# Zero fills and mask rows planned as tasks, identity made in bf16 by GpSimd, first loads reordered, boot weights booked at 300 GB/s

## Chip, cores, metric

One core of one Trainium2 chip. The metric is the device time of one execution in microseconds (us). PE is TensorE, DVE VectorE, ACT ScalarE, POOL GpSimd, SP the SyncE queue that issues the loads; PEld is PE's loading of weights.

## The reference

Two transformer-like layers, each a recurrent attention with memory (A) and a gated feed-forward (B), both layers with the same weights:

```python
def _A_ref(x, mem0, Wq, Wk, Wv, Wo, seg_len):       # 2048 rows, 64 segments of 32, 32 heads of 128
    mem = mem0                                       # 8 rows
    for s in range(n_seg):
        h = concatenate([mem, x[:, s*seg_len:(s+1)*seg_len]], axis=1)      # 40 rows
        q, k, v = h@Wq, h@Wk, h@Wv
        p = softmax(where(mask, q@k.T * scale, -1e9))
        o = (p @ v) @ Wo
        mem = o[:, :M]                               # the next segment waits for this
        outs.append(o[:, M:])
x = x + _A_ref(_layernorm(x), ...);  x = x + _B_ref(_layernorm(x), ...)
x = x + _A_ref(_layernorm(x), ...);  x = x + _B_ref(_layernorm(x), ...)
```

## The kernel before

All work is given as tasks to a planner written in Python. It knows each task's engine, booked duration and dependencies, runs 24 rounds of list scheduling and fixes one order of instructions for each engine. On the chip every engine then works through its order and goes on as soon as its semaphores allow; the booked times have no part in that. So a booked number changes the order, never a duration.

The constants were made outside the plan, in an order chosen by the framework:

```python
def setup_consts(self):
    identf = fview(self.st[1][:, 0, 0:1], [(1, P)])
    cmasks.make_identity(nc, identf)                          # f32, GpSimd
    nc.vector.tensor_copy(out=self.ident[:], in_=identf)      # cast to bf16, VectorE
    ...                                                       # masks by GpSimd, small memsets by VectorE
    nc.sync.dma_start(out=self.maskb[L:LW, :], in_=self.mask1[:])
    for t_ in self.hT: nc.vector.memset(t_[:, :, L:2 * L], 0.0)
    for t_ in self.pb: nc.vector.memset(t_[:], 0.0)
    for k, t_ in enumerate(self.vsb):                         # five tiles of 128 x 1024 bf16
        self.pl.add("POOL", 950, lambda t_=t_: nc.gpsimd.memset(t_[:], 0.0), w=[...])
```

The boot loads 16 MiB of weights while PE projects V for the first twelve blocks of x ("V fill", line 570) and, as each group of six heads comes in, does Q and K of step 0:

```python
def load_weights(self):
    for h0 in range(0, self.H, 8):                            # Wv in four pieces of 1 MiB
        ld(self.wv[:, :, cs], ..., P * self.DC * 8 * P * 2 / 300.0, ...)
        for b in xb[:3]: self.load_x(b, *self.boot_x[b])
        xb = xb[3:]
    for g, (h0, gsz, us) in enumerate(self.groups):           # five groups of 6 heads, one of 2
        for nm, sb, v in (("wq", self.wq, wq_v), ("wk", self.wk, wk_v)):
            ld(sb[:, :, cs], v[:, :, cs], nb / 260.0, ...)    # booked ns: bytes / (GB/s)
        ld(self.wo[:, h0:h0 + gsz, :], ..., P * gsz * self.D * 2 / 200.0, ...)

def boot(self):                                               # priority of a boot load
    self.nboot = getattr(self, "nboot", 0) + 1
    return 1e7 - 1e4 * self.nboot

def layernorm_T(self, xb, xkey, ...):                         # bn_stats, bn_aggr, +eps on VectorE,
    ...                                                       # pow(-0.5) on GpSimd, normalise on VectorE,
                                                              # four transposes on PE with the identity
```

## Time and profile before

| | before |
|---|---|
| time, median (lowest to highest) | 1872.28 us (1869.12 to 1873.32), 3 runs |
| span of the profiled run | 1869.7 us |
| PE busy | 1822.6 us, 97% |
| PE idle, 0 to 20 us / 20 to 90 us / after 90 us | 10.7 / 0.9 / 35.5 us |
| first V matmul | 11.65 us |

The idle time of PE is the span less its busy time; the stretches come from the windows view. Not all of it is idle: this trace lacks 214 of PE's 41282 matmul records. Windows of before, from 120 to 150 us (stretch, length, busy us of PE, PEld, DVE, ACT, POOL with counts, granted clock, DMA share, GB/s):

```profile
120.00:130.00 10.00, 8.78 (x249) 7.65 (x246) 7.71 (x29) 6.10 (x23) 2.60 (x4) 1.00 0.26 69
140.00:150.00 10.00, 9.42 (x246) 8.52 (x243) 5.44 (x22) 5.58 (x20) 0.00 (x0) 0.66 0.13 35
```

PE lacks 1.2 us of 120 to 130, and in 140 to 150 the granted clock is 0.66: the trace's clock records have half clock (PE's array granted half of its full clock) from 142.0 to 148.8 us.

### The profile page before, as it was taken

Reading aid. Unit: us, or ns where it says so; the run is one execution under the profiler, and the core shown is the slowest. Engines: PE = TensorE matmul, PEld = TensorE weight load, DVE = VectorE, ACT = ScalarE, POOL = GpSimd, SP = SyncE. Lnnn points to the kernel's source line nnn. Section 1 sums busy time; section 2 is a strip of 40 time slices with the busy share of each in tenths; the row PEclk is TensorE's granted clock in tenths of the full one; section 3 lists DMA queues with packets and bytes.
Section 4 is the critical chain, followed back from the end, with each engine's and each line's share of the span. In section 5 each row is a group of like instructions: output and inputs, shape, how many; then the busy total and the mean of one; then the engine's idle time right before and its main releaser. Section 6 shows DMA issues by size and latency. Waiting matters only on the chain.

```text
span 1869.7 us, 94235 instructions
## 1 busy us (share of the span) xinstructions
PE 1822.6 (97%) x41068; PEld 1577.4 (84%) x41282; DVE 1282.3 (69%) x4167; ACT 1137.3 (61%) x2692; POOL 583.2 (31%) x832
## 2 busy tenths in 40 slices
PE   7999999999999999999999999999999999999999
PEld 3578788888989898989988898989889898988787
DVE  5366577776777667776677677666777677766565
ACT  4655556666666666566666666666666666666554
POOL 5412012332423232333323233233323232333323
PEclk9999999999999999999999999999999999999999
DMA  9733334554645544555545554555545454455534
GB/s 354 247 102 103 89 86 119 153 155 129 182 124 153 151 143 124 151 151 149 166 128 152 147 143 131 141 152 153 157 121 152 136 156 122 141 152 145 158 100 138
DMA packets 130060, 273.83 MB, mean 146 GB/s; under 512 B 29254, under 2 KB 60750, under 8 KB 129646
## 3 DMA queue, kind: packets, MB, share of 16 engines
q0 software_dynamic: 59984, 184.49, 33.7%
q1 hardware_dynamic: 69662, 83.30, 15.5%
q8 instruction: 323, 5.29, 1.2%
q14 instruction: 91, 0.75, 0.1%
HBM read 221.85 MB, written 27.26 MB: 133 GB/s over the span
## 4 chain that ended last, share of the span: by engine, by line
PE 92%; DVE 4%; ACT 2%; issue 1%; DMA 0%; POOL 0%; SPq 0%; ACTq 0%; DVEq 0%; POOLq 0%
PE bank L708 32%; PE bank L811 16%; PE bank L910 11%; PE bank L570 9%; PE bank L680 7%; PE bank L722 5%; PE bank L781 4%; PE bank L794 4%; PE bank L934 4%; PE bank L540 1%; DVE st L735 1%; ACT otsb L1002 1%; DVE pb L764 0%; DMA vsb<-sst 0%; PE bank L878 0%
## 5 line engine op out<-in xcount | busy, mean ns | idle before, releaser
L708 PE MATMUL bank<-hT,wq_sb 128*128 128x80 bf16 (+1 forms) x8960 | 624.2, 198 | 5.7 <-issue 1.7
L708 PE MATMUL bank<-hT,wk_sb 128*128 128x80 bf16 (+1 forms) x8960 | 622.9, 198 | 1.4 <-issue 1.4
L1002 ACT CAST qku<-bank 128x480 bf16<-128x480 f32 (+3 forms) x770 | 393.9, 512 | 265.5 <-PE bank L708 253.3
L708 PEld LDWEIGHTS <-wq_sb 128*128 128x128 bf16 x8960 | 458.1, 99 | 27.9 <-issue 8.5
L708 PEld LDWEIGHTS <-wk_sb 128*128 128x128 bf16 x8960 | 450.7, 99 | 1.6 <-issue 1.6
L735 DVE TENSOR_TENSOR st<-bank,maskb 80x240 f32<-80x240 f32 (+1 forms) x732 | 268.7, 368 | 234.5 <-PE bank L722 227.7
L811 PE MATMUL bank<-otsb,wo_sb 128*128 128x80 bf16 (+1 forms) x8960 | 371.8, 198 | 7.4 <-ACT otsb L1002 5.5
L811 PEld LDWEIGHTS <-wo_sb 128*128 128x128 bf16 x8960 | 339.7, 99 | 21.5 <-issue 10.3
L902 POOL DMA_DIRECT2D wg<-in_B_w_gate_dram x217 | 165.0, 760 | 489.4 <-PE bank L910 419.7
L1002 ACT CAST otsb<-bank 128x480 bf16<-128x480 f32 (+3 forms) x420 | 200.8, 486 | 76.7 <-PE bank L794 61.9
L928 POOL DMA_DIRECT2D wd<-in_B_w_down_dram x217 | 153.7, 710 | 256.6 <-PE bank L794 98.5
L764 DVE TENSOR_TENSOR pb<-st,rz 80x480 bf16<-80x480 f32 x348 | 205.8, 592 | 3.5
L745 ACT ACTIVATE st<-st 80x240 f32<-80x240 f32 (+3 forms) x420 | 159.8, 382 | 64.6 <-DVE st L742 62.7
L1002 ACT CAST ptsb<-bank 128x480 bf16<-128x480 f32 (+3 forms) x315 | 155.3, 499 | 65.2 <-PE bank L781 62.9
L530 POOL TENSOR_TENSOR lns<-lns,negh 128x1 f32<-128x1 f32 (+1 forms) x79 | 45.4, 576 | 449.0 <-DVE lns L529 334.7
L722 PE MATMUL bank<-qku 128*80 128x80 bf16 (+1 forms) x2240 | 176.7, 202 | 1.8 <-ACT qku L1002 0.4
L747 DVE TENSOR_REDUCE sm<-st 80x6 f32<-80x240 f32 (+3 forms) x420 | 151.7, 362 | 35.5 <-ACT st L745 33.4
L910 PE MATMUL bank<-xnT,wg 128*128 128x128 bf16 (+2 forms) x1784 | 171.8, 219 | 1.5 <-ACT xnT L1002 0.2
L910 PE MATMUL bank<-xnT,wu 128*128 128x128 bf16 (+2 forms) x1784 | 171.2, 218 | 0.1
L722 PEld LDWEIGHTS <-qku 128*80 128x80 bf16 (+1 forms) x2240 | 129.9, 117 | 46.2 <-issue 11.5
L903 POOL DMA_DIRECT2D wu<-in_B_w_up_dram x217 | 162.5, 749 | 4.6 <-PE bank L781 1.4
L742 DVE TENSOR_TENSOR st<-st,mx 80x240 f32<-80x240 f32 (+3 forms) x420 | 155.7, 371 | 3.9
(98 smaller groups left out, 2475.1 us busy)
## 6 DMA issues: line engine op xcount, KB each, us to landing
wg<-in_B_w_gate_dram POOLq DMA_DIRECT2D x220, 256.0 KB, 4.3
wu<-in_B_w_up_dram POOLq DMA_DIRECT2D x220, 256.0 KB, 4.7
wd<-in_B_w_down_dram POOLq DMA_DIRECT2D x220, 256.0 KB, 5.2
vsb<-scr SPq DMA_DIRECT2D x508, 48.0 KB
vsb<-sst SPq DMA_DIRECT2D x280, 64.0 KB
scr<-vst SPq DMA_DIRECT2D x128, 96.0 KB
wv_sb<-in_A_Wv_dram SPq DMA_DIRECT2D x4, 1024.0 KB
wq_sb<-in_A_Wq_dram SPq DMA_DIRECT2D x5, 768.0 KB
```

Of the source, the lines that this page charges most:

```text
L570: nc.tensor.matmul(B[:, :], lhsT=tile[:, c, :], rhs=self.wv[:, c, cs], start=(c == 0), stop=(c == DC - 1))
L708: nc.tensor.matmul(o_ap, lhsT=W[:, c, h * P:(h + 1) * P], rhs=mv(c), start=(c == 0), stop=(c == DC - 1))
L722: nc.tensor.matmul(s_all(SB)[pr, uh - h0 + i, :], lhsT=qku[:, i, 0, 0:ncol], rhs=qku[:, i, 1, 0:ncol], start=True, stop=True)
L735: pl.add("DVE", dve_ns(n, True), lambda gsz=gsz, hs=hs, st=st, SB=SB, pj_=pj_, npj_=npj_, mk=mk, idx=idx: nc.vector.tensor_tensor(out=st[p ...
L742: pl.add("DVE", dve_ns(n), lambda gsz=gsz, hs=hs, st=st, mx=mx: nc.vector.tensor_tensor(out=st[pr, hs], in0=st[pr, hs], in1=mx[pr, hs].uns ...
L745: pl.add("ACT", act_ns(n), lambda hs=hs, st=st: nc.scalar.activation(out=st[pr, hs], in_=st[pr, hs], func=ACTF.Exp, scale=self.scale), r=s ...
L764: nc.vector.tensor_tensor(out=o, in0=st[pr, hs].unsqueeze(1).to_broadcast([npart, 2, gsz, L]), in1=rz[pr, :, 0:gsz].unsqueeze(3).to_broadc ...
L811: nc.tensor.matmul(WB[:, c * ncol:(c + 1) * ncol], lhsT=self.wo[:, h, c * P:(c + 1) * P], rhs=otsb[:, hl, 0:ncol], start=(h == 0 and c == ...
L902: pl.add("POOL", 760, lambda wg=wg, fs=fs: nc.gpsimd.dma_start(out=wg[:], in_=self.wgv[:, :, fs]), r=[("wo", self.H - 1)], w=[gk] + bt, la ...
L903: pl.add("POOL", 760, lambda wu=wu, fs=fs: nc.gpsimd.dma_start(out=wu[:], in_=self.wuv[:, :, fs]), r=[("wo", self.H - 1)], w=[uk] + bt, la ...
L910: nc.tensor.matmul(gu[:, 2 * i + k, 0:n], lhsT=W[:, c, i * P:(i + 1) * P], rhs=xnT[:, c, rw], start=(c == 0), stop=(c == DC - 1))
L1002: nc.scalar.copy(out=dst, in_=src)
```

## The change

Intent: let the first layernorm start as soon as x is there, not behind constants; let the planner see the zero fills; ask for x before Wv; and book the weights' loads at a truer rate. Cut to its core:

```diff
 def setup_consts(self):
-        identf = fview(self.st[1][:, 0, 0:1], [(1, P)])
-        cmasks.make_identity(nc, identf)
-        nc.vector.tensor_copy(out=self.ident[:], in_=identf)
+        cmasks.make_identity(nc, self.ident[:])
 ...
-        nc.sync.dma_start(out=self.maskb[L:LW, :], in_=self.mask1[:])
-        for t_ in self.hT: ...  for t_ in self.pb: ...  for k, t_ in enumerate(self.vsb): ... gpsimd.memset
+    def clear(self):
+        pl.add("SP", 430, lambda: nc.sync.dma_start(out=self.maskb[L:LW, :], in_=self.mask1[:]), w=["maskb"])
+        for k, t_ in enumerate(self.hT): pl.add("DVE", 120, ... memset ...)
+        for k, t_ in enumerate(self.pb): pl.add("DVE", 400, ... memset ...)
         for k, t_ in enumerate(self.vsb):
+            if k == 0:
+                pl.add("DVE", 550, lambda t_=t_: nc.vector.memset(t_[:], 0.0), w=keys)
+            else:
+                pl.add("ACT", 960, lambda t_=t_: nc.scalar.copy(out=t_[:], in_=self.vsb[0][:]), r=[("vs", 0)], w=keys)
 def load_weights(self):
-        for h0 in range(0, self.H, 8):
+        for h0, n in ((0, 4), (4, 4), (8, 8), (16, 8), (24, 8)):        # first piece of Wv halved
-                ld(sb[:, :, cs], v[:, :, cs], nb / 260.0, ...)          # Wq, Wk
-            ld(self.wo[...], ..., P * gsz * self.D * 2 / 200.0, ...)
+                ld(sb[:, :, cs], v[:, :, cs], nb / 300.0, ...)
+            ld(self.wo[...], ..., P * gsz * self.D * 2 / 300.0, ...)
 def trace(self):
-        self.load_mem0()
+        self.clear()
         p0 = self.pre1(0); p1 = self.pre1(1)                            # loads of x0, x1
 ...
+        self.load_x(2, *self.boot_x[2])
+        self.load_mem0()
         self.load_weights()
 def run(self):
-        self.setup_consts()
         self.trace()
         order = self.pl.plan()
         with self.tc.manual_schedule():
+            self.setup_consts()
```

The rest of the diff: the first loads are booked with a latency of 2.5 us in place of 4, and the mask addition reads the key `maskb` when two layers run together.

More of the change, by code (lines that the diff above doesn't have):

```diff
@@ L465, in setup_consts @@
         nc.vector.memset(self.jm[0:L, 1:2], 0.0)
-        for t_ in self.hT:
-            nc.vector.memset(t_[:, :, L:2 * L], 0.0)
-        for t_ in self.pb:
-            nc.vector.memset(t_[:], 0.0)
-        for k, t_ in enumerate(self.vsb):
-            self.pl.add("POOL", 950, lambda t_=t_: nc.gpsimd.memset(t_[:], 0.0), w=[("vs", k), ("vx", 0, k), ("vx", 1, k)])
+    def clear(self):
+        nc, pl = self.nc, self.pl
+        pl.add("SP", 430, lambda: nc.sync.dma_start(out=self.maskb[L:LW, :], in_=self.mask1[:]), w=["maskb"])
+        for k, t_ in enumerate(self.hT):
+            pl.add("DVE", 120, lambda t_=t_: nc.vector.memset(t_[:, :, L:2 * L], 0.0), w=[("hT", k, 1, q) for q in ("m", "x")])
+        for k, t_ in enumerate(self.pb):
+            pl.add("DVE", 400, lambda t_=t_: nc.vector.memset(t_[:], 0.0), w=[("pb", k)])
+        for k, t_ in enumerate(self.vsb):
+            keys = [("vs", k), ("vx", 0, k), ("vx", 1, k)]
+            if k == 0:
+                pl.add("DVE", 550, lambda t_=t_: nc.vector.memset(t_[:], 0.0), w=keys)
+            else:
+                pl.add("ACT", 960, lambda t_=t_: nc.scalar.copy(out=t_[:], in_=self.vsb[0][:]), r=[("vs", 0)], w=keys)
     def load_weights(self):
@@ L481, in ld @@
             pl.add("SP", ns, lambda: nc.sync.dma_start(out=dst, in_=src), w=keys, boost=self.boot())
-        xb = list(self.boot_x)
-        for h0 in range(0, self.H, 8):
-            cs = slice(h0 * P, (h0 + 8) * P)
-            ld(self.wv[:, :, cs], wv_v[:, :, cs], P * self.DC * 8 * P * 2 / 300.0, [("wv", h) for h in range(h0, h0 + 8)])
+        xb = list(self.boot_x)[1:]
+        for h0, n in ((0, 4), (4, 4), (8, 8), (16, 8), (24, 8)):
+            cs = slice(h0 * P, (h0 + n) * P)
+            ld(self.wv[:, :, cs], wv_v[:, :, cs], P * self.DC * n * P * 2 / 300.0, [("wv", h) for h in range(h0, h0 + n)])
+            if h0 == 0:
+                continue
             for b in xb[:3]:
@@ L493, in load_weights @@
             for nm, sb, v in (("wq", self.wq, wq_v), ("wk", self.wk, wk_v)):
-                ld(sb[:, :, cs], v[:, :, cs], nb / 260.0, [(nm, h) for h in range(h0, h0 + gsz)])
-            ld(self.wo[:, h0:h0 + gsz, :], wo_v[:, h0:h0 + gsz, :], P * gsz * self.D * 2 / 200.0, [("wo", h) for h in range(h0, h0 + gsz)])
+                ld(sb[:, :, cs], v[:, :, cs], nb / 300.0, [(nm, h) for h in range(h0, h0 + gsz)])
+            ld(self.wo[:, h0:h0 + gsz, :], wo_v[:, h0:h0 + gsz, :], P * gsz * self.D * 2 / 300.0, [("wo", h) for h in range(h0, h0 + gsz)])
     def boot(self):
@@ L504, in load_mem0 @@
         m0 = self.xo[0][0:MEM, :]
-        pl.add("SP", 100, lambda: nc.sync.dma_start(out=m0, in_=self.mem0), w=[("xo", 0)], boost=self.boot())
+        pl.add("SP", 100, lambda: nc.sync.dma_start(out=m0, in_=self.mem0), w=[("xo", 0)], lat=2500.0, boost=self.boot())
         B = pl.buf(self.bank, "bg")
@@ L622, in pre1 @@
         xb = self.xs[i]
-        pl.add("SP", 430, lambda: nc.sync.dma_start(out=xb[:], in_=self.x_in[b * P:(b + 1) * P, :]), w=[("xs", i)], boost=(self.boot() if b < 2 else 0))
+        pl.add("SP", 430, lambda: nc.sync.dma_start(out=xb[:], in_=self.x_in[b * P:(b + 1) * P, :]), w=[("xs", i)], lat=2500.0 if b < 2 else None, boost=(self.boot() if b < 2 else 0))
         self.xw[(0, b)] = i
@@ L737, in emit_step @@
                     in1=mk[pj_, :].unsqueeze(1).to_broadcast([npj_, gsz, L]), op=ALU.add),
-                    r=[SB] + ([("st", gi, 0)] if both and j == 0 else []), w=[("st", gi, 0), ("st", gi, 1)])
+                    r=[SB] + ([("st", gi, 0)] if both and j == 0 else []) + (["maskb"] if both else []), w=[("st", gi, 0), ("st", gi, 1)])
             sk = [("st", gi, 0), ("st", gi, 1)]
```

## The prediction

> **What bounds the kernel now.** I read the page first, then busy time by windows, then the timeline of the first 24 us, then PE's waits and the SP queue. The page says that TensorE (PE) is busy for nearly the whole span, and that only the first of 40 slices is poor:
>
> ```profile
> PE 1822.6 (97%) x41068; PEld 1577.4 (84%) x41282; DVE 1282.3 (69%) x4167; ACT 1137.3 (61%) x2692; POOL 583.2 (31%) x832
> PE   7999999999999999999999999999999999999999
> PE 92%; DVE 4%; ACT 2%; issue 1%; DMA 0%; POOL 0%; SPq 0%; ACTq 0%; DVEq 0%; POOLq 0%
> ```
>
> The chain that ended last is 92% PE. So the time is PE's work, about 1822.6 us, plus PE's idle time, 1869.7 - 1822.6 = 47.1 us. The change takes no matmul away, so it can gain only in those 47 us. The windows say where they lie (columns: stretch, its length, then busy us of PE, PEld, DVE, ACT, POOL, granted clock, DMA share, GB/s):
>
> ```profile
> 0.00:10.00 10.00, 0.74 (x8) 0.60 (x8) 7.72 (x26) 1.28 (x1) 6.75 (x18) 1.00 0.78 262
> 10.00:20.00 10.00, 8.54 (x39) 3.74 (x38) 6.54 (x23) 5.13 (x14) 4.10 (x8) 1.00 1.06 374
> 20.00:30.00 10.00, 9.89 (x72) 4.43 (x72) 3.51 (x10) 5.74 (x10) 8.11 (x14) 1.00 1.07 385
> 60.00:70.00 10.00, 9.89 (x100) 5.19 (x100) 3.14 (x10) 6.30 (x13) 5.28 (x10) 1.00 0.97 317
> 70.00:80.00 10.00, 9.84 (x105) 5.54 (x105) 4.53 (x11) 5.46 (x12) 5.04 (x10) 1.00 0.64 187
> ```
>
> The first 20 us hold 10.7 us of idle PE. From 20 to 90 us, while weights arrive at up to 385 GB/s, PE lacks only 0.9 us of 70, because the V projections (line 570) fill it. From 90 us on the remaining 35 us of idle time are spread thinly over the recurrence and its end, which the change does not edit. The timeline of the first microseconds (start, duration, engine, line) shows why PE starts late:
>
> ```profile
> 1.21 0.84 SPq L623 DMA_DIRECT2D xs<-in_A_x_dram  x2
> 1.78 1.19 DVE L469 MEMSET pb<- 80x384 uint32 x3
> 3.00 3.38 DVE L451 CAST ident<-st 128x128 bf16<-128x128 f32 x1
> 3.57 2.73 POOL L471 MEMSET vsb<- 128x1024 bf16 x3
> 6.43 0.24 PE L513 MATMUL bank<-ident,xo 8*128 8x8 bf16 x4 [6.43 <-DVE ident L451]
> 6.81 1.28 DVE L527 BATCH_NORM_STATS2 lns<-xs 128x6 f32<-128x512 bf16 x2
> 9.50 0.61 PE L540 MATMUL bank<-ident,xn 128*128 128x128 bf16 x4 [2.82 <-DVE xn L531]
> 11.65 3.60 PE L570 MATMUL bank<-wv_sb,xvf 128*128 128x512 bf16 x8 [0.36 <-ACT xvf L1002]
> 16.20 2.76 PE L570 MATMUL bank<-wv_sb,xvf 128*128 128x512 bf16 x12 [0.53 <-ACT xvf L1002]
> ```
>
> What to see: casting the identity to bf16 occupies VectorE from 3.00 to 6.38 us, which is absurd for 128 elements a row. GpSimd's zero fills of vsb end at 6.30, and the cast ends 0.08 us later. Only then do the statistics of the first layernorm begin (6.81), and the first useful matmul follows 4.84 us after them, at 11.65.
>
> **What the Trainium skill says.** "SBUF — State Buffer", section "SBUF: two separate sides", says that VectorE and GpSimd share a port pair as an exclusive lock held for a whole instruction, and names an fp32 copy between SBUF tiles as an operation that takes it. The trace agrees as far as it goes: the cast lasts exactly as long as the GpSimd fills (0.08 us over), although VectorE's own memsets beside the first fill (0.12 us each) are undisturbed. "VectorE: DVE Perf Modes", section "Zero memsets can be issued as uint32 (trn2)", says that a memset takes one cycle per element and that a bf16 zero fill can be issued as half as many uint32. The trace agrees: 384 uint32 took 0.38 us. "TensorE: Matmul & The Clock Gate", section "What's actually happening", says that the array runs at half its clock for about 3.4 us of its first sustained work. The trace shows that as well: the first 8 matmuls of 512 columns took 3.60 us (0.45 each), the next 12 took 2.76 us (0.23 each). The page's granted clock reads 1.00 there, so that row does not show it. This price is paid before and after; it starts sooner when PE starts sooner.
>
> **Part by part.**
> (1) Identity in bf16 by GpSimd. Removes the cast of 3.38 us and its wait. Memset and select were 0.20 + 0.29 us in f32, so the identity is ready at about 1.3 us. Beside other work, on no path.
> (2) Zero fills. GpSimd loses five fills of 0.94 us. VectorE gets one of 512 uint32, by the row of pb 0.38 x 512/384 = 0.5 us; ScalarE gets four copies, planned at 0.96 us. ScalarE's first real work was at 10.15 us, its table load ended at 2.03, so the 3.8 us lie in a hole; at worst one copy holds up the first eviction by under 1 us. VectorE has then, before the statistics: five tiny memsets until about 1.15, eight of hT (0.58/6 each, 0.8 us), three of pb (1.19 us), one of vsb (0.5 us), so it is free at about 1.15 + 2.5 = 3.65 us. The plan will put them there: it books 0.96 + 1.2 + 0.55 = 2.7 us for them and x at 2.93.
> (3) Loads. x0 is issued at 0.75 rather than 1.21. The 8 KB of mem0, issued at 0.75, released PE's weight load at 2.39, so 1.64 us; 128 KB at 371 GB/s (the rate in the fifth microsecond) add 0.35 us. Estimate: x0 landed at 3.2 before and at 2.75 after. It was never what the statistics waited for. The first half megabyte of Wv follows three x blocks and is in by about 5.5 us, before PE can use it. The mask row's transfer leaves the front of the SP queue, where it had waited 0.6 us for GpSimd.
> So the statistics start at max(2.75, 3.65) = 3.65, not 6.81: 3.2 us sooner. With the measured 4.84 us from there, the first V matmul comes at 8.5, not 11.65. Block 2 now arrives before Wv rather than behind it, so I take back half of the 0.9 us that PE idles between 15.28 and 16.20: 0.5 us. Sum on the path: 3.7 us.
> (4) Boot weights planned at 300 GB/s. This moves no byte, it only changes where the planner puts Q/K work among the V fill. Three transfers of 768 KB are booked as 7.9 us in place of 10.0. Adding up the SP queue's bytes in the trace, the Q/K weights of the six head groups are in at about 24, 33, 42, 51, 60 and 62 us; PE uses them at 32.6, 42.9, 53.7, 64.0, 73.6 and 80.1. So they lay waiting for 9 to 19 us. With 2.1 us less per group the use moves to roughly 28, 37, 45, 53, 61 and 65: still behind the arrivals, the fifth by about 1 us. Step 0 ends some 12 us sooner and V fill is left over for steps 1 to 5, where PE idled 3.9 us between 100 and 200 us. I take 0.8 us for it.
> Total 3.7 + 0.8 = 4.5 us: 1872.3 - 4.5 = 1867.8 us, or 0.24%.
>
> **The rivals.**
> *The new plan gives it back.* Every position after the boot is planned again from other numbers, and the order of several thousand tasks can fall better or worse. For it: PE's thin idle time after 90 us is 35 us, and a tenth more or less of it is 3.5 us, as much as the gain. Against: the tasks are the same and the planner keeps the best of 24 rounds. It would make 1864 to 1872, and I expect this term to decide how close I am.
> *DMA bounds the boot.* If the last weights set the end of step 0, a sooner start only means waiting for them. For it: DMA share 1.06 from 10 to 60 us, and the SP queue blocks on issue (one Wq transfer took 5.82 us to be accepted):
>
> ```profile
> 24.78 5.82 SPq L481 DMA_DIRECT2D wq_sb<-in_A_Wq_dram  x1
> 53.12 4.04 SPq L481 DMA_DIRECT2D wq_sb<-in_A_Wq_dram  x1
> 59.13 2.11 SPq L481 DMA_DIRECT2D wo_sb<-in_A_Wo_dram  x1
> ```
>
> Against: PE was at 98% and more in those stretches, and used weights long after they came. But 300 GB/s is over what the queue gave in fact: a Wq issue ended every 9.1 us on average (20.7, 30.6, 40.2, 48.1, 57.2), that is 2.36 MB at 259 GB/s, with the scratch writes beside it. If the new order asks too early, PE waits in place and idles 2 to 4 us between 45 and 65 us, and the time stays at 1870 to 1872.
> *The fills come late.* If VectorE's or ScalarE's fills land in front of the statistics or of the first evictions, the start is at 9.5 rather than 8.5, and the time is 1869.
>
> **Range and chances.** Centre 1867.8. The front is sure to 1 us, the weights' order to 2, the new plan to 4; together about 5 us each way, with somewhat more room below since the planner now has truer numbers: 1860 to 1873.5. Two per cent would be 37 us, nearly all of the idle time that there is; so faster 0.01, slower 0.01, same 0.98.
>
> **What would show it right or wrong.** In the profile after: no cast of the identity; statistics of x at about 3.7 us; first line-570 matmul at 8 to 9 us, with slow matmuls for the 3.5 us behind it; PE busy in 0 to 20 us up from 9.3 to some 12.8; Q/K of the fifth group near 61 us without an idle stretch over 1 us before it; PE's busy total the same within 2 us of 1822.6. Wrong if the start moves by less than 2 us, if PE waits for weights between 40 and 70 us, or if idle time after 90 us moves from 35 us by more than 4.

## The result

| | before | after |
|---|---|---|
| first comparison, median (range) | 1872.53 (1869.12 to 1873.32), 4 runs | 1870.62 (1869.75 to 1871.98), 4 runs |
| ratio, 95% interval | | 0.9994, 0.9977 to 1.0011 |
| span of the profiled run | 1869.7 | 1868.4 |
| PE idle, 0 to 20 / 20 to 90 / after 90 us | 10.7 / 0.9 / 35.5 | 8.7 / 1.2 / 38.2 |
| first V matmul | 11.65 | 8.60 |

A ratio here is the mean time of one kernel's fast runs over that of the other's of the same rounds, so it is not quite the ratio of the medians. The two later comparisons of the same kernel gave 0.9987 (0.9975 to 1.0000) and 0.9995 (0.9981 to 1.0009). In means that is 1.1, 2.3 and 1.3 us less (4, 6 and 6 runs), weighted by runs 1.7 us, or 0.09%. "Same" in the sense of 2%; most likely a little faster.

The page after, the lines that answer to those of before (busy, the 40 slices of PE, the chain that ended last):

```profile
PE 1820.4 (97%) x41062; PEld 1575.1 (84%) x41282; DVE 1282.3 (69%) x4175; ACT 1140.0 (61%) x2688; POOL 576.6 (31%) x821
PE   8999999999999999999999999999999999999998
PE 88%; DVE 3%; SPq 3%; DMA 2%; issue 2%; ACT 1%; POOL 0%; ACTq 0%; DVEq 0%; POOLq 0%
```

PE's share of the chain has fallen by four points, and SPq (the queue that issues the loads) and DMA, both 0% before, now have five. The windows after:

```profile
0.00:10.00 10.00, 2.87 (x16) 1.30 (x16) 6.99 (x35) 6.95 (x12) 2.98 (x14) 1.00 0.78 264
10.00:20.00 10.00, 8.47 (x42) 3.84 (x42) 4.62 (x16) 4.19 (x8) 5.70 (x10) 1.00 1.06 382
60.00:70.00 10.00, 9.51 (x109) 5.00 (x108) 3.32 (x11) 6.13 (x13) 4.55 (x8) 1.00 1.00 330
140.00:150.00 10.00, 9.34 (x284) 7.82 (x281) 6.41 (x23) 4.34 (x16) 7.15 (x11) 1.00 0.55 156
```

The first 10 us gained 2.1 us of PE, the second 10 us nothing, 60 to 70 us lost 0.4; the half clock near 142 us is gone. The timeline after of the first microseconds:

```profile
0.74 0.87 SPq L631 DMA_DIRECT2D xs<-in_A_x_dram  x2
1.02 0.29 POOL masks.py:199 TENSOR_SCALAR_AFFINE_SELECT ident<-ident 128x128 bf16<-128x128 bf16 x1
2.42 0.48 DVE L475 MEMSET vsb<- 128x512 uint32 x1
2.94 3.88 ACT L477 COPY vsb<-vsb 128x1024 bf16<-128x1024 bf16 x4 [0.92 <-DVE vsb L475]
3.66 1.29 DVE L535 BATCH_NORM_STATS2 lns<-xs 128x6 f32<-128x512 bf16 x2
8.60 1.89 PE L578 MATMUL bank<-wv_sb,xvf 128*128 128x512 bf16 x4 [0.45 <-ACT xvf L1012]
13.60 1.33 POOL L1008 DMA_DIRECT2D scr<-wd  x2 [4.83 <-ACT wd L1012]
16.03 0.40 PE L548 MATMUL bank<-ident,xn 128*128 128x128 bf16 x4 [1.48 <-DVE xn L539]
```

The identity is done at 1.31, the fills of vsb lie where the prediction put them, the statistics start at 3.66 (forecast 3.65) and the first V matmul at 8.60 (forecast 8.5). The last two lines are a wait that nobody had forecast: GpSimd issues two transfers of V results to a scratch tensor (scr) from 13.60, the pow of the next layernorms stands behind them in its order although its input was ready at 13.56, and PE idles 1.48 us until 16.03. Before, the order was the other way round, and PE lost 0.53 us there. The two lines of GpSimd in before, then its pow in after:

```profile
13.90 1.58 POOL L530 TENSOR_TENSOR lns<-lns,negh 128x1 f32<-128x1 f32 x3 [4.38 <-DVE lns L529]
16.17 1.33 POOL L998 DMA_DIRECT2D scr<-wd  x2 [0.69 <-ACT xvf L1002]
```

```profile
14.95 1.60 POOL L538 TENSOR_TENSOR lns<-lns,negh 128x1 f32<-128x1 f32 x3
```

**Lead.** Times of one kernel spread over 4 to 7 us on one chip, so most of what follows is read from traces. The lead of a kernel is how much sooner than in the trace of before PE does the same work. PE's 41282 weight loads are numbered from the end; in all traces their sequence is the same from 245 us of before on, so past that the lead compares the same instruction with itself. In between the orders differ. But one place near the start has equal work in front of it in every trace: the first V matmuls from hT ("strips", line 680 of before) come after 56 V matmuls, 20 transposes of x and 4 of mem0, whatever the order of these. In before and in after:

```profile
27.11 1.91 PE L680 MATMUL bank<-wv_sb,hT 128*32 128x512 bf16 x32
```

```profile
25.21 1.91 PE L688 MATMUL bank<-wv_sb,hT 128*32 128x512 bf16 x32
```

So the lead at 27 us is 1.9 us. (At the first Q/K matmul, 32.41 against 29.65, it seems to be 2.8; but after has done four V matmuls fewer by then.) At 290 us the lead of the profiled after is 3.3 us; at 1790 us it is 2.6 and at the end 1.3.

### The profile page after: what moved, and what is told of

Same layout as the page of the kernel before. It is cut to its first block, busy times and chain, and to the rows that moved or that the text cites. A ratio compares the mean times of both kernels' runs of the same rounds, so it can differ in the third digit from the quotient of the medians.

```text
span 1868.4 us, 94225 instructions
## 1 busy us (share of the span) xinstructions
PE 1820.4 (97%) x41062; PEld 1575.1 (84%) x41282; DVE 1282.3 (69%) x4175; ACT 1140.0 (61%) x2688; POOL 576.6 (31%) x821
## 4 chain that ended last, share of the span: by engine, by line
PE 88%; DVE 3%; SPq 3%; DMA 2%; issue 2%; ACT 1%; POOL 0%; ACTq 0%; DVEq 0%; POOLq 0%
PE bank L716 31%; PE bank L819 16%; PE bank L918 11%; PE bank L688 7%; PE bank L578 7%; PE bank L730 5%; PE bank L789 4%; PE bank L802 4%; PE bank L942 4%; SPq L487 2%; PE bank L548 1%; DVE st L743 1%; DMA vsb<-sst 1%; ACT otsb L1012 1%; DMA wk_sb<-in_A_Wk_dram 1%
## 5 line engine op out<-in xcount | busy, mean ns | idle before, releaser
L819 PEld LDWEIGHTS <-wo_sb 128*128 128x128 bf16 x8960 | 339.0, 99 | 22.0 <-issue 10.7
```

The source lines that it names most:

```text
L819: nc.tensor.matmul(WB[:, c * ncol:(c + 1) * ncol], lhsT=self.wo[:, h, c * P:(c + 1) * P], rhs=otsb[:, hl, 0:ncol], start=(h == 0 and c == ...
```

## The experiments

My theory after reading the traces, which the experiments bore out only in part: the sooner start is worth its length, and what is missing from the sum was lost where weights are asked for as they land (theory W). The rivals: the sooner start is swallowed (B of e1), the new rates are gain on paper only (B of e3), or the run-to-run scatter hides the whole 4.5 us.

All results first. "Wk wait" is what PE waited for Wk in the first 130 us; "half clock" is a half-clock record between 100 and 200 us.

| kernel | lead at 27 us | lead at 290 us | Wk wait | half clock | time against before of the same rounds: means, ratio and interval |
|---|---|---|---|---|---|
| aa_before (trace) | 0.0 | -0.8 | none | 141.8 to 152.0 | |
| e1_ident_only | 2.2 | 2.2 | none | 139.8 to 146.6 | -1.2; 0.9994 (0.9982 to 1.0006) |
| e6_fills_only | 2.9 | 1.9 | none | 141.7 to 148.5 | -1.7; 0.9990 (0.9976 to 1.0005) |
| e2_delay | -7.5 | -7.9 | none | 139.0 to 142.4, 152.6 to 156.0 | +5.8; 1.0031 (1.0018 to 1.0044) |
| e4_after_oldrates | 1.9 | 0.8 | none | 139.5 to 146.3 | -2.3; 0.9988 (0.9976 to 1.0000) |
| e3_before_newrates | 0.4 | 3.4 | none | none | -3.0; 0.9984 (0.9972 to 0.9996) |
| e3_again | 0.0 | 1.8 (3.0 at 230 us) | none | none (240.9 to 244.3) | -1.9; 0.9991 (0.9978 to 1.0003) |
| after | 1.9 | 3.3 | 0.4 | none | -1.1; 0.9994 (0.9977 to 1.0011) |
| after_again | 2.6 | 2.5 | 2.1 | none | -2.3; 0.9987 (0.9975 to 1.0000) |
| after_third | 1.9 | 4.1 | 0.2 | none | -1.3; 0.9995 (0.9981 to 1.0009) |
| e5_strict_order | 2.4 | 3.1 | 1.2 | none | -0.2; 0.9999 (0.9986 to 1.0012) |
| e7_warm | 2.1 | 2.0 | 1.1 | none | +0.9; 1.0005 (0.9989 to 1.0022) |
| e8_warm_r270 | 1.9 | 4.0 | none | none | +0.2; 1.0002 (0.9989 to 1.0014) |

### e1_ident_only: before, the identity in bf16 and nothing else

```diff
-        identf = fview(self.st[1][:, 0, 0:1], [(1, P)])
-        cmasks.make_identity(nc, identf)
-        nc.vector.tensor_copy(out=self.ident[:], in_=identf)
+        cmasks.make_identity(nc, self.ident[:])
```

> The kernel before with only the identity made in bf16 by GpSimd; the cast is gone, the plan and every engine's later order are those of before. In the trace the statistics of x should begin near 3.3 us in place of 6.81 and the first V matmul near 8.2 in place of 11.65. Theory A (a sooner start is worth its full length at the end): 3 to 3.5 us less than before, ratio 0.998. Theory B (the sooner start is swallowed by later waits for weights or scratch): lead of PE's instructions shrinks to under 1 us by 250 us, ratio 0.9995 to 1.000.

Timeline of this kernel:

```profile
3.33 1.29 DVE L525 BATCH_NORM_STATS2 lns<-xs 128x6 f32<-128x512 bf16 x2 [0.16 <-DMA xs<-in_A_x_dram]
3.57 2.73 POOL L469 MEMSET vsb<- 128x1024 bf16 x3
6.28 1.07 POOL L528 TENSOR_TENSOR lns<-lns,negh 128x1 f32<-128x1 f32 x2
9.48 3.60 PE L568 MATMUL bank<-wv_sb,xvf 128*128 128x512 bf16 x8 [0.36 <-ACT xvf L1000]
```

The statistics came at 3.33 as expected, the first V matmul only at 9.48, not 8.2: the pow that they feed stands behind the vsb fills on GpSimd and begins at 6.28, when the last fill ends. So the fills on GpSimd held the start twice, through the cast on VectorE and through GpSimd's own order; taking the cast away cures one. The lead is 2.17 us at 10 us and 2.24 at 540 us, with the same order throughout: a sooner start passes on undiminished (A), at least through the boot; by 640 us 0.4 us of it is left, for reasons that the part on aa_before shows. The time, 1.2 us less, cannot tell 2.2 from 0.

### e6_fills_only: before, the vsb fills off GpSimd and nothing else

```diff
         for k, t_ in enumerate(self.vsb):
-            self.pl.add("POOL", 950, lambda t_=t_: nc.gpsimd.memset(t_[:], 0.0), w=[...])
+            if k == 0: self.pl.add("DVE", 550, lambda t_=t_: nc.vector.memset(t_[:], 0.0), w=keys)
+            else: self.pl.add("ACT", 960, lambda t_=t_: nc.scalar.copy(out=t_[:], in_=self.vsb[0][:]), r=[("vs", 0)], w=keys)
```

> The kernel before with only the five vsb fills moved from GpSimd to VectorE and ScalarE as in after; the f32 identity and its cast stay. If it was the GpSimd fills that held VectorE, the cast shrinks from 3.38 us to under 0.3 and the first V matmul comes at 8.3 to 9 us, as in after, although the cast is still there; rival: the cast itself is slow or waits for something else, then it stays over 3 us. Time: 2 to 4 us less than before if the start passes through.

```profile
3.54 0.23 DVE L451 CAST ident<-st 128x128 bf16<-128x128 f32 x1
9.03 3.33 PE L574 MATMUL bank<-wv_sb,xvf 128*128 128x512 bf16 x8 [0.36 <-ACT xvf L1006]
```

The same cast on the same tile takes 0.23 us in place of 3.38 once GpSimd fills nothing. That shows that the fills held it, and the first V matmul at 9.03, 2.6 us sooner, shows that moving the fills is the greater part of the front. Its lead of 2.9 us shrinks to 1.9 by 290 us; this plan's order of PE differs from before's between 56 and 128 us, and nothing was run to say where in it the 1.0 us went.

### e2_delay: before, held up in front on purpose

```diff
+        for _ in range(26):
+            nc.vector.memset(self.pb[0][:], 0.0)
         nc.vector.tensor_copy(out=self.ident[:], in_=identf)
```

> The kernel before with 26 more zero fills of one pb tile on VectorE (26 x 0.397 = 10.3 us) ahead of the identity's cast, on purpose; plan and later order unchanged. The cast then starts at 13.3 us with GpSimd idle and takes about 0.2 us, so PE's first matmul comes at 13.6, not 6.43: 7 us late. Theory A (the start passes to the end one for one): 6.5 to 7.5 us slower, ratio 1.0037. Theory B (V fill waits for weights anyway, so part is swallowed): 3 us or less slower. In between, 4 to 6, if Wv and x, all landed by then, let the first passes run without the pauses of before.

The framework put some fills behind the cast and between the statistics, so the first PE matmul was on time and the layernorms were late. (The cast began at 4.96, beside GpSimd's fills, and again ended at 6.37, 0.07 us after the last of them, while VectorE's memsets ahead of it ran on at 0.38 us each: it is the cast that is held, not VectorE at large.) V began 4.8 us late and PE was 7.5 us behind at 20 us:

```profile
13.81 0.61 PE L542 MATMUL bank<-ident,xn 128*128 128x128 bf16 x4 [7.14 <-DVE xn L533]
16.46 3.39 PE L572 MATMUL bank<-wv_sb,xvf 128*128 128x512 bf16 x8 [0.86 <-ACT xvf L1004]
```

The lead is -7.5 us at 27 us, -7.9 at 290 us and the time 5.8 us longer (interval 3.4 to 8.2 us: 0.0018 and 0.0044 of 1873). Theory A holds: what the start loses, the end loses. In this kernel's own plan there is no slack behind the start. It is the clearest result in the times.

### e3_before_newrates and e3_again: before, the booked rates and nothing else

```diff
-                ld(sb[:, :, cs], v[:, :, cs], nb / 260.0, ...)
-            ld(self.wo[...], ..., P * gsz * self.D * 2 / 200.0, ...)
+                ld(sb[:, :, cs], v[:, :, cs], nb / 300.0, ...)
+            ld(self.wo[...], ..., P * gsz * self.D * 2 / 300.0, ...)
```

> The kernel before with only the booked rates of the Wq, Wk and Wo loads at 300; the late start at 11.65 us stays. The planner's own sum falls by 4.8 us. Theory A (truer rates let the chip gain what the planner books): 3 to 5 us less than before. Theory B (the booked gain is idle time that the chip never had, since engines run on as soon as data is there; the new order only asks for weights earlier): within 1.5 us of before, and up to 2 us more, with PE idle just ahead of Q/K matmuls between 45 and 70 us.

> The kernel before with the new rates alone, again, now beside the whole change on one chip. If the parts added up, after would be 3 us faster than this. Theory W (not additive: the last groups' Q/K start when Wk lands, in either): the two are within 1.5 us of each other, and the Q/K of the last two heads start within 1.5 us of each other (69.8 against 68.8 and 70.2 us in the traces so far).

Three booked numbers, with the cast and the late start left as they were, gave 3.0 and 1.9 us less; the first interval excludes 1. The lead grows from 0.4 to 3.4 us, and in the second trace from 0.0 to 3.0 at 230 us: 3.0 us each time. (The 0.4 goes with a shorter half clock in the first trace: full clock was granted at 14.2 us against 15.7. A half clock at 240.9 us takes 1.2 us of the second trace's lead.) So the new rates are not gain on paper, though they bring three of the planner's 4.8 us. Where: PE is busy 9.88 us between 120 and 130 in place of 8.78, and there is no half clock near 142 us. That stretch is in all six traces with the old rates (before, aa_before, e1, e2, e4, e6), in e1 2.2 us sooner just as its whole program is, in e2 as two shorter ones, and in none of the eight with new rates (300, or 270 in e8). It belongs to the old rates' orders, not to the run. That the thinner PE work ahead of it causes it is likely but was not tried by itself, nor was how much of the 3.0 us is owed to it.

### e4_after_oldrates: after, the booked rates of before

```diff
-                ld(sb[:, :, cs], v[:, :, cs], nb / 300.0, ...)
-            ld(self.wo[...], ..., P * gsz * self.D * 2 / 300.0, ...)
+                ld(sb[:, :, cs], v[:, :, cs], nb / 260.0, ...)
+            ld(self.wo[...], ..., P * gsz * self.D * 2 / 200.0, ...)
```

> The kernel after with the booked rates of before (260 and 200), the rest of the change kept. Theory A: slower than after by 2 to 4 us, near 1873. Theory B: as fast as after or faster by up to 3 us, 1868 to 1870, since the start at 8.6 us stays and PE no longer waits for weights near 60 us.

Trace and time disagree. In the trace the half clock is back (139.5 to 146.3 us), there is no wait for Wk, and the lead falls from 1.9 to 0.8 us, 2.5 less than after has at 290 us: as theory A says. It falls although nothing waits for weights, as in e6: a new plan on the old rates gave back 1.0 and 1.1 us of the sooner start (e1, which keeps the order of before, gave back none). The time, 2.3 us less than before, is as good as that of after in the same rounds. With intervals of 2.2 us each way the time does not decide; by itself this experiment is inconclusive.

### after_again, after_third: the whole change twice more

> The kernel after once more, for more rounds on the same chip as the others and for a second trace. 1 to 2 us less than before, ratio 0.9985 to 1.000. If the stretch of half clock in the trace of before (142.0 to 148.8 us) is a matter of the run and not of the kernel, such a stretch may show here too or elsewhere.

> The kernel after a third time, beside the next three on one chip. 1.5 to 3 us less than before.

What PE waits for in the boot, in after_again and then in after:

```profile
39.30 0.27 PE L716 MATMUL bank<-hT,wk_sb 128*128 128x40 bf16 x4 [1.70 <-DMA wk_sb<-in_A_Wk_dram]
```

```profile
68.81 0.27 PE L716 MATMUL bank<-hT,wk_sb 128*128 128x40 bf16 x4 [0.44 <-DMA wk_sb<-in_A_Wk_dram]
```

Before, with its late start and its slow booked rates, never waited for a weight. Now PE stands before the second group's Wk in one run and before the last two heads' in another, and how long differs: 0.4, 2.1 and 0.2 us. The trace's semaphore records, which no view of the profile lists, show why: a load raises its semaphore 16 times, and the 16th is its landing. Wk of the last two heads landed at 68.8, 70.1 and 68.7 us in these three, just when PE began with it, and between 66.1 and 70.1 us in all fourteen traces, sooner start or not. In after the 15th part was there at 65.9, so that wait is for one late part of sixteen. In e3, with the late start, the Q/K of the last two heads begin at 69.8 and 70.2 us without a wait, Wk having landed at 66.1 and 67.3. So the landing bounds the sooner start, as theory W says, but not e3, and it costs 0.2 to 2.1 us.

From 27 to 290 us the lead changes by +1.4, -0.1 and +2.2 us in the three traces of after. Adding the wait for Wk back gives 1.8, 2.0 and 2.4 (1.9 in e5, 2.1 in e8, but 1.0 in e7): most of the difference between the three is of the size of that wait.

### e5_strict_order: after, loads kept in named order

In after the planner had put Wo of the first group and two blocks of x between Wk of the first group and Wk of the second; steps of 10 us between priorities did not keep the named order, steps of 1000 us (below) did.

```diff
-        return 1e7 - 1e4 * self.nboot
+        return 1e8 - 1e6 * self.nboot
```

> The kernel after with the boot loads kept in the order in which the program names them (Wq, Wk, Wo of each group), by larger steps of their priority, all else as in after. In after the SP queue put Wo and two x blocks ahead of Wk of group 1, and PE waited 0.4 us (first trace) and 2.1 us (second trace) for Wk. Theory W (the sooner start is partly eaten by weights that are asked for as they land): no wait of PE for Wk over 0.3 us, and 0.5 to 2 us less than after, 1868 to 1869.5. Rival: those waits are slack that later idle time absorbs; same as after within 0.5 us (1870).

The wait did not go away, it moved: PE waited 1.2 us for Wk before the fifth group, at 62.5 us. The lead at 290 us is 3.1, that of after. My expectation that the queue's order was at fault missed. In the named order, too, Wo and the x blocks stand ahead of the second group's Wk, only sooner, and it landed at 36.4 us against 36.0 in after.

### e7_warm: after, with the array warmed up

```diff
         cmasks.make_identity(nc, self.ident[:])
+        for _ in range(45):
+            nc.tensor.matmul(self.bank.tiles[7][:, 0:P], lhsT=self.ident[:], rhs=self.ident[:], start=True, stop=True)
```

> The kernel after with 45 matmuls on the identity into an unused PSUM bank in front, while PE has nothing to do (1.4 to about 6 us); plan and order of the rest unchanged. In after the V matmuls ran at half clock from 8.60 to 12.8 us, 4.2 us, so 2.1 us are lost there. Theory C (cold array is a real term of the start): full clock is granted before or soon after 8.6 us, PE leads after by 1 to 2 us at 20 us; how much of it is left at 290 us says whether weights take it: Theory W says under 0.7 us, and a longer wait for Wk near 60 to 70 us. Rival: array cools again between the identity matmuls and the V matmuls, then no lead at 20 us.

Windows of one us of this kernel:

```profile
7.00:8.00 1.00, 0.42 (x8) 0.23 (x4) 0.78 (x3) 0.79 (x3) 0.00 (x0) 1.00 1.10 380
9.00:10.00 1.00, 1.00 (x3) 0.30 (x2) 0.34 (x3) 0.53 (x2) 0.00 (x0) 0.50 1.05 386
12.00:13.00 1.00, 1.00 (x7) 0.40 (x5) 1.00 (x4) 0.46 (x1) 0.00 (x0) 1.00 1.05 383
```

The array was at full clock from 5.2 us, went back to half clock at 8.6, after PE had been mostly idle from 6 on (0.26 and 0.42 us busy of 6 to 7 and 7 to 8), and ran the first V matmuls at half clock until 12.0. Lead over after at 20 us: 0.2. The rival holds. Whether work without that gap would have kept the clock was not tried. The later lead (2.0 at 290 us) has Wk waits of 1.1 us in it.

### e8_warm_r270: the attempt at a better version

The same 45 matmuls, the loads in named order as in e5, and 270 in place of 300 for all three booked rates.

> The kernel after with the same 45 matmuls, loads in named order and booked at 270 in place of 300, so that Q/K of the last groups is asked for about 1 us per group later. Theory W: no wait for Wk over 0.3 us, lead over before 3.5 to 5 us at 290 us, 1867.5 to 1869.5 us. Rival (planner booked 1 us more for it, so it is no better): as after, 1870.

No wait for Wk at all, and the lead at 290 us is 4.0, the highest but for after_third. So far theory W. But the time is that of before, 0.2 us more: the lead melts to 2.0 by 640 us, 0.7 by 890 us and nothing by 1790 us, much of it in steps at short pauses of PE that are the subject of the next part. No version beat both kernels; e3, the booked rates alone, did as well as the whole change in both comparisons on the same chip (1869.15 against 1869.74, and 1870.76 against 1871.27).

### aa_before: how much two runs of the same program differ

> The kernel before itself, for a second trace. If the half clock near 142 us belongs to the program it is here again within 1 us of 142.0, and the two traces' leads differ only by short pauses of about 1 us at differing places; if it is a matter of the run, it is elsewhere or missing.

With the same order the second trace is level until 140 us, 0.8 us behind at 290 (its half clock lasted 10.2 us, not 6.8), 2.7 behind at 1790 and 3.9 at the end. The steps come at pauses like these, in before and then in after, at nearly the same place of the program, the first 1.4 us later in time:

```profile
1072.48 0.30 PE L708 MATMUL bank<-hT,wq_sb 128*128 128x80 bf16 x4 [0.94 <-issue]
```

```profile
1071.09 0.21 PE L716 MATMUL bank<-hT,wq_sb 128*128 128x80 bf16 x1 [1.22 <-issue]
```

"issue" means that PE waited for nothing that the profile shows. Between 240 and 1840 us the fourteen traces have 6 to 12 pauses of over 0.5 us, together 4.3 to 8.2 us. Five of them are in every trace at the same place and of the same length, and have a cause that the profile names: waits for ScalarE or VectorE of 0.65 us near 315, 1.04 near 318, 0.70 near 370 and 0.58 near 426 and 742. Most of those that differ from run to run are of the kind "issue", 1 to 5 in each trace, 0.8 to 4.0 us together, at recurring places (near 541, 961, 1071, 1175, 1329, 1384).

The packed trace shows what these are, though no view lists it. The queue of instructions (q8 on the page) brings 323 packets of 16384 bytes, and 324 in e7 and e8, which have 45 matmuls more, so it carries PE's program. In all fourteen traces each of the 43 "issue" pauses ends 1.3 to 1.7 us after such a packet has landed; of the 85 pauses with a named cause 3 do, and of PE's matmuls at large 9%. So PE stands because its next instructions come late. This is read from times alone; why a packet is late in one run and not in another, no run shows.

And the drain differs: eleven of the fourteen traces have half clock for 3.4 or 6.8 us from 1844 to 1853 us, while before, after and e6 kept full clock until the last few us. The trace of before that everything is compared with is a lucky one: timed at 1871.5 us against a mean of 1872.6 for its 37 timed runs, with no half clock and no such pause after 1840. From 1790 us to the end every other trace loses 0.7 to 2.8 us of lead against it, which is why leads of 3 us at 290 us end as spans only 1 us shorter.

## Why the prediction was right or wrong

Right: the range held (1870.62 in 1860 to 1873.5), the time stayed within 2%. The size was too large: 4.5 us forecast, 1.1, 2.3 and 1.3 measured in three comparisons. What failed is the size of the front: 3.7 us were forecast, and the lead at equal work is 1.9, 2.6 and 1.9 us. That the rates brought more than forecast covered part of this, which was luck.

- **What holds VectorE.** Right, and shown by e6: 3.38 to 0.23 us. The prediction missed that the same fills also held the pow in GpSimd's own order (e1: 9.48 and not 8.2). It did not hurt, since the change moves the fills and makes the identity at once.
- **Start of the statistics and of V.** 3.65 and 8.5 forecast, 3.66 and 8.60 measured.
- **"I take back half of the 0.9 us".** This is the step that failed. PE gained nothing in the second 10 us (8.47 us busy against 8.54): it waited 1.48 us for the pow behind two scratch issues, 1.62 and 1.23 in the other traces, where before had waited 0.53. Of the 3.05 us by which V starts sooner, 1.15 are gone at 27 us, and this wait is 0.95 of them. The new order of GpSimd did that: e6, in which pow stays ahead of the scratch issues, starts V 0.43 us later than after and yet leads by 2.9 us at 27. No run changes this order alone.
- **That the start reaches the end.** Right to 540 us where it was tested with an unchanged order: e1 keeps 2.2 us, e2 -7.9 to -8.0. Later pauses blur it, and the time of e2 (3.4 to 8.2 us longer) is the only one that shows it.
- **0.8 us for the booked rates.** Mis-sized. Alone they are worth 3.0 us of lead (e3, twice), and the half clock near 142 us is gone with them. That line was in the windows before (0.66), and the prediction passed over it.
- **"The new plan gives it back."** This rival came true in part: with the old rates, new plans lost 1.0 and 1.1 us (e6, e4), which the sum had at nothing.
- **"DMA bounds the boot."** So did this one: 0.2 to 2.1 us of waiting for Wk in place of the 2 to 4 feared. The arrivals that the prediction had added up from the queue's bytes, 24, 33, 42, 51, 60 and 62 us, were too early: in the trace of before Wk of the six groups landed at 25.9, 36.3, 44.9, 52.7, 61.9 and 67.9.
- **The sum.** Front, new plan (e4), rates alone (e3) and wait for Wk give 1.9 - 1.1 + 3.0 - 0.4 = 3.4 us for the profiled after, and 2.4 and 3.6 for the other two; 3.3, 2.5 and 4.1 were measured at 290 us. So the parts add up within 0.5 us. This is arithmetic after the fact, with terms of one or two traces each, and two traces of before differ by 0.8 us there. In times the parts do not add: e4 and e3 gained 2.3 and 3.0 us, the whole 2.3 in the same rounds; with intervals of 2.2 us each way that decides nothing.
- **What is left at 290 us and missing in the time.** On average 3.3 us of lead against 1.7 us of time. The three traces of after still average 3.5 us at 1790; the rest goes in the drain, where the trace of before was lucky, so part of the loss is in the reference. e5, e7 and e8 had leads of 2.0 to 4.0 and times like before's; why is open.
- **The announced signs.** PE busy in 0 to 20 us: 12.8 forecast, 11.3 measured. Fifth group near 61 us: 63.2. PE busy total within 2 us: 2.2 less; the half clock that is gone would do that, but the trace also has six matmul records fewer. Idle after 90 us within 4 us of 35: 38.2, in both with missing records.

## What to carry to other kernels

A fill or cast that looks free can hold the start through a shared port and through an engine's own order: look at an instruction whose duration is absurd for its size, and at what ended when it ended. When a new order starts an engine sooner, look at what now stands in front of the next link of the chain on every engine, GpSimd's issues included. When two parts of a change both make the same data wanted sooner, ask when that data lands. When a gain is below the scatter, number the instructions and compare traces, but only where the same work lies behind them; and one reference trace may itself be a lucky one. Where a pause has no releaser, look at the instruction queue's packets.

## What the Trainium skill lacked or had wrong

- "SBUF — State Buffer", section "SBUF: two separate sides", speaks of the loser being blocked for the winner's whole instruction. Here the cast began at 3.00, and was not served at the change from one GpSimd instruction to the next either: fills from 2.61, 3.57 (three) and a small memset at 3.50, which follow each other without a gap in the trace, all went first, and it ended at 6.38, 0.08 us after the last; 3.38 us in place of the 0.23 of e6. VectorE's memsets ran on beside those fills at 0.38 us each (e2).
- "TensorE: Matmul & The Clock Gate", section "What's actually happening", ties half clock to an idle window of about 3.4 us. The lengths agree (3.4, 6.8 and 10.2 us here, and 3.4 us in e7), the idle window does not: in before half clock was granted at 142.0 us although no gap between matmuls in the 22 us ahead of it was over 0.45 us (nor in aa_before, which has every record) and PE was busy 8.78 and 9.63 us of 120 to 130 and 130 to 140. A later section of that page, "A second HAM failure mode: psum-queue depth-cycling", speaks of short idle times between groups of matmuls that bring it about, without lengths; here the longest were 0.45 us.
- "Runtime: NRT & Kernel Launch", section "Instruction fetch mechanics", has the fetch of straight-line code mostly hidden and names taken branches as what stalls. Here PE stood 43 times for over 0.5 us (0.8 to 4.0 us a trace between 240 and 1840 us), each time until 1.3 to 1.7 us after a packet of 16384 bytes of its instructions had landed.
